# Top-32 attention and a leaky-ReLU MLP on one core: the order of the queries, the engines of the masks and the pairing of heads are changed

## The chip, the core and the metric

The kernel runs on one core of a Trainium2 chip, in one launch. The metric is the device time of an execution in microseconds (us); smaller is better. Three executions of the kernel before took 2387.86, 2389.12 and 2391.31 us, so the median is 2389.12 us. The engines are named as in the profile: PE (TensorE matmul) and PEld (its weight loads), DVE (VectorE), ACT (ScalarE), POOL (GpSimd), SP (SyncE, which issues the DMAs here).

## What is computed

All data are float32, except that the two MLP weights arrive as float64 and are rounded to float32 on the chip.

```python
# q, k, v: (8 batches, 8 heads, 576 rows, 64)
scores = (1 / sqrt(64)) * q @ k.T                   # 576 x 576 for each head
kth    = the 32nd largest of each row
scores = where(scores >= kth, scores, -1e9)
attn   = exp(scores - max);  attn = attn / (sum(attn) + 1e-9)
x      = (attn @ v), heads side by side             # 4608 tokens x 512
h      = x @ w_in                                   # 512 x 2048
out    = max(0.01 * h, h) @ w_out                   # 2048 x 512
```

## The kernel before

A pair is two neighbouring heads of a batch; there are 32 pairs, four to a batch, and a pair fills 128 rows of x. The queries of a pair (2 x 576 rows) are cut into nine tiles of 128 rows, 288 tiles in all; the middle tile (t == 4) holds 64 rows of either head. For each tile `softmax_tile` makes the scores on PE (L140: the contraction is 64 long, in two halves of 288 keys), copies them out on ACT (L147, tile s_sb), and finds the 32 largest of each row on DVE: four times MAX8 (L155) and between them three times MATCH_REPLACE8 (L160), which overwrites the eight just found. Each step needs the one before. ACT takes the exponents (L158); DVE masks and sums them in one instruction (L166) and makes the reciprocal (L171, L173); ACT scales the row (L174).

`transpose_tile` turns a tile over on PE, four blocks of 128 keys (L181) and one of 64 (L183), and ACT copies them to wT (L185, L186). When a head is complete, `weigh_values` multiplies it with v, in two halves of 288 queries and five chunks of keys (L196), and ACT copies the result into x (L203).

The tiles of two batches make a group (72 tiles, 1152 tokens). `mlp` works on a complete group in chunks of 384 tokens: for each of 16 blocks of d_ff, four matmuls (L212), a copy by ACT (L217), and the leaky ReLU by DVE (L218); then for each 128 tokens 16 matmuls (L225), a copy (L232) and a store. It is a generator, and the main loop takes its steps in even parts between the tiles of the next group, so the MLP runs a whole group behind, and the last group's MLP has no attention beside it.

A float32 matmul is two passes on PE, so counts of matmuls in the profile are twice those of the code (transposes are one pass).

The weights are loaded in 32 chunks of 128 x 512 during the first group, one to every two tiles, and rounded by `convert_weights`, ten DVE instructions to a chunk (L97 to L108). The loads of q, k and v of the next pair (six DMAs) and the stores are issued by SP. The order of each engine's instructions is chosen by the framework's scheduler from the program's dependencies and priorities; the code fixes none.

Of the kernel before, what the change touches and what calls it, by code (L numbers as in the profile page):

```python
# [8 lines left out]
F32 = mybir.dt.float32  # L9
# [3 lines left out]


@with_exitstack
def kernel(
# [4 lines left out]
    v: bass.AP,  # L21
# [7 lines left out]
    NPAIR, D, _, S = qT.shape  # L29
    B, H = v.shape[0], v.shape[1]  # L30
    DFF, DMODEL = moe_w_out.shape[0], moe_w_in.shape[0]
    P = 128
# [4 lines left out]
    assert D == 64 and S == 576 and H % 2 == 0 and DMODEL == H * D  # L37

    HS = S // 2  # a row of scores is two halves, one PSUM bank each
    NKC = 5  # chunks of keys: four of 128 and one of 64  # L40
    KLEN = [P, P, P, P, S - 4 * P]
    TPP = 2 * S // P  # 128-row query tiles of a pair; the middle one holds rows of both heads
    HP = H // 2  # pairs of a batch = 128-row chunks of d_model
    NFC = DFF // P
    GB = 2  # batches of a token group
    GTOK = GB * S
    CHT = 384  # tokens of an MLP chunk
    NGRP = B // GB
    TILES_PER_GROUP = GB * HP * TPP
    WCH = 512  # columns of a chunk of weights  # L50
    LAG = 2  # tiles by which the transposes run behind the scores
# [3 lines left out]
    loads = ctx.enter_context(tc.tile_pool(name="loads", bufs=2))  # L55
    work = ctx.enter_context(tc.tile_pool(name="work", bufs=2))
    small = ctx.enter_context(tc.tile_pool(name="small", bufs=4))
    ps_sc = ctx.enter_context(tc.tile_pool(name="ps_sc", bufs=2, space=bass.MemoryType.PSUM))
# [8 lines left out]
    gT = [const.tile([P, CHT], F32, name=f"gT{f}") for f in range(NFC)]  # L67

    def weight_chunks():
        """(destination, source) of 128 rows and 512 columns each"""  # L70
        words = moe_w_in.shape[1] // DFF
        for c in range(HP):
            for j in range(DFF // WCH):
                yield (w_in[c][:, j * WCH:(j + 1) * WCH],
                       moe_w_in[c * P:(c + 1) * P, j * WCH * words:(j + 1) * WCH * words])
        for f in range(NFC):
            for j in range(DMODEL // WCH):
                yield (w_out[f // 4][:, f % 4, j * WCH:(j + 1) * WCH],
                       moe_w_out[f * P:(f + 1) * P, j * WCH * words:(j + 1) * WCH * words])

    def load_weights(dst, src):
        """Starts a chunk's load; what convert_weights takes, if it has yet to be rounded."""
# [3 lines left out]
        raw = loads.tile([P, WCH, 2], U32, name="raw")  # L86
# [3 lines left out]
    def convert_weights(dst, raw):  # L90
        """float64 words to the nearest float32: the sign, the exponent and the leading 23 bits
        of the mantissa by bits, then the other 29 bits added as a float. Past float32's range
        it gives no finite number, and below its least normal one something below that."""
        lo, hi, bits = raw[:, :, 0], raw[:, :, 1], dst.bitcast(U32)
        ex = work.tile([P, WCH], U32, name="ex", tag="tmp")
        rem = work.tile([P, WCH], U32, name="rem", tag="tmp")
        nc.vector.tensor_scalar(ex, hi, 20, 0x7FF, ALU.logical_shift_right, ALU.bitwise_and)  # L97
        nc.vector.tensor_scalar(ex, ex, 896.0, 1151.0, ALU.max, ALU.min)
        nc.vector.tensor_scalar(ex, ex, -896.0, 8388608.0, ALU.add, ALU.mult)
        nc.vector.tensor_scalar(bits, hi, 3, 0x7FFFF8, ALU.logical_shift_left, ALU.bitwise_and)  # L100
        nc.vector.scalar_tensor_tensor(out=bits, in0=lo, scalar=29, in1=bits,
                                       op0=ALU.logical_shift_right, op1=ALU.bitwise_or)
        nc.vector.tensor_tensor(bits, bits, ex, ALU.bitwise_or)
        nc.vector.tensor_scalar(rem, lo, 0x1FFFFFFF, None, ALU.bitwise_and)
        nc.vector.scalar_tensor_tensor(out=ex.bitcast(F32), in0=rem, scalar=2.0 ** -52,  # L105
                                       in1=ex.bitcast(F32), op0=ALU.mult, op1=ALU.mult)
        nc.vector.tensor_tensor(dst, dst, ex.bitcast(F32), ALU.add)
        nc.vector.scalar_tensor_tensor(out=bits, in0=hi, scalar=0x80000000, in1=bits,  # L108
                                       op0=ALU.bitwise_and, op1=ALU.bitwise_or)

    def load_pair(pi):
        b, h0 = divmod(2 * pi, H)
        qt = loads.tile([D, 2, S], F32, name="qt")
        kt = loads.tile([D, 2, S], F32, name="kt")
        vt = loads.tile([P, 2, NKC, D], F32, name="vt")
        nc.sync.dma_start(qt, qT[pi])
        nc.sync.dma_start(kt, kT[pi])
        for side in range(2):
            nc.sync.dma_start(
                vt[:, side, 0:4, :],  # L120
                v[b, h0 + side, 0:4 * P, :].rearrange("(c p) d -> p c d", p=P),
            )
            nc.sync.dma_start(vt[0:KLEN[4], side, 4, :], v[b, h0 + side, 4 * P:S, :])
        return qt, kt, vt

    def tile_parts(t):
        """(head of the pair, first query, first row of the tile, rows)"""
        if t < 4:
            return [(0, P * t, 0, P)]
        if t == 4:  # L130
            return [(0, 4 * P, 0, 64), (1, 0, 64, 64)]
        return [(1, 64 + P * (t - 5), 0, P)]

    def softmax_tile(pair, t):
        """Normalized top-k weights of one tile of queries, [query, key]."""
        qt, kt, _ = pair
        psc = ps_sc.tile([P, 2, 512], F32, name="psc")
        for side, q0, r0, rows in tile_parts(t):
            for half in range(2):
                nc.tensor.matmul(  # L140
                    psc[r0:r0 + rows, half, 0:HS],
                    qt[:, side, q0:q0 + rows],
                    kt[:, side, half * HS:(half + 1) * HS],
                    start=True, stop=True,
                )
        s_sb = work.tile([P, S], F32, name="s_sb")
        nc.scalar.copy(s_sb.rearrange("p (h n) -> p h n", h=2), psc[:, :, 0:HS])  # L147

        tops = small.tile([P, TOPK // 8, 8], F32, name="tops")
        rest = work.tile([P, S], F32, name="rest", bufs=1)  # L150
        nbias = small.tile([P, 1], F32, name="nbias")
        e_sb = work.tile([P, S], F32, name="e_sb")
        src = s_sb
        for r in range(TOPK // 8):
            nc.vector.max(out=tops[:, r, :], in_=src)  # L155
            if r == 0:
                nc.vector.tensor_scalar(nbias, tops[:, 0, 0:1], -SCALE, None, ALU.mult)  # L157
                nc.scalar.activation(e_sb, s_sb, AF.Exp, bias=nbias, scale=SCALE)  # L158
            if r + 1 < TOPK // 8:
# [169 lines left out]
```

## Time and profile before

| | |
|---|---|
| executions | 2387.86, 2389.12, 2391.31 us (median 2389.12) |
| profiled execution, first to last instruction | 2387.1 us |
| PE busy | 2090.5 us (88%) |
| DVE busy | 1996.9 us (84%) |
| ACT busy | 984.9 us (41%) |
| POOL busy | 0.7 us |
| mean granted PE clock | 0.890 of full speed |

The profile gives the profiled execution's span and no separate time for it; the three timed executions are 0.8 to 4.2 us longer than that span. Busy time is the union of an engine's instructions; an instruction's mean duration is longer than the distance to the next one's start, since neighbours overlap at their ends. [...]

### The profile page before, as it was taken

The numbers are of one execution on the slowest core, as the hardware profiler recorded it, in microseconds if no ns is written. First come the engines' busy times: TensorE is split into PE (matmuls) and PEld (weight loads), VectorE is DVE, ScalarE is ACT, GpSimd is POOL, SyncE is SP. The second block draws the span as 40 slices with busy tenths as digits, with TensorE's granted clock in tenths as the row PEclk, the third lists the DMA queues.
The fourth block names the chain that finished last, engine by engine and source line by source line (L and its number), as shares of the span: only waits on it lengthen the run. The fifth ranks groups of instructions, "written<-read, shape, count | busy, mean of one in ns | idle before, by whom it ended". The sixth has DMA issues, their size and how long they took to land.

```text
span 2387.1 us, 21604 instructions
## 1 busy us (share of the span) xinstructions
PE 2090.5 (88%) x6688; PEld 1051.6 (44%) x6688; DVE 1996.9 (84%) x4832; ACT 984.9 (41%) x1861; POOL 0.7 (0%) x6
## 2 busy tenths in 40 slices
PE   5665666568999999999999999996899999986999
PEld 2232332234445454454454545543444545543554
DVE  8999998998889898888898898998898888998200
ACT  3333333334444454444444444444444444443110
POOL 0000000000000000000000000000000000000000
PEclk9665665557999999999999999996899999996999
DMA  3111111110000000000001000010000000000000
GB/s 77 38 42 45 42 41 41 45 42 5 20 24 16 19 20 20 24 15 15 20 16 29 13 22 20 16 28 15 10 16 24 16 24 18 17 14 0 0 14 13
DMA packets 53939, 55.93 MB, mean 23 GB/s; under 512 B 41024, under 2 KB 41024, under 8 KB 53824
## 3 DMA queue, kind: packets, MB, share of 16 engines
q1 hardware_dynamic: 53824, 54.54, 8.4%
q8 instruction: 54, 0.88, 0.2%
q14 instruction: 61, 0.50, 0.1%
HBM read 45.09 MB, written 9.44 MB: 23 GB/s over the span
## 4 chain that ended last, share of the span: by engine, by line
PE 67%; DVE 29%; ACT 3%; issue 1%; DMA 0%; DVEq 0%; SPq 0%; ACTq 0%
PE pz L225 20%; PE ph L212 15%; PE po L196 15%; PE psc L140 11%; DVE tops L155 11%; DVE rest L160 8%; PE main L181 4%; DVE w_sb L166 4%; ACT s_sb L147 1%; PE tail L183 1%; DVE gT L218 1%; DVE ex L105 1%; ACT h_sb L217 1%; ACT e_sb L158 0%; ACT wT L185 0%
## 5 line engine op out<-in xcount | busy, mean ns | idle before, releaser
L140 PE MATMUL psc<-kt,qt 64*128 64x288 f32 (+1 forms) x1280 | 459.0, 496 | 266.7 <-ACT s_sb L147 259.3
L155 DVE MAX8 tops<-rest 128x8 f32<-128x576 f32 x864 | 650.8, 753 | 12.7
L212 PE MATMUL ph<-x,w_in 128*128 128x384 f32 x1536 | 536.8, 493 | 2.9 <-ACT x L203 1.9
L225 PE MATMUL pz<-w_out,gT 128*128 128x512 f32 x1152 | 534.7, 601 | 0.0
L140 PEld LDWEIGHTS psc<-kt,qt 64*128 64x128 f32 (+1 forms) x1280 | 220.7, 203 | 492.6 <-ACT s_sb L147 354.2
L160 DVE MATCH_REPLACE8 rest<-tops,rest 128x576 f32<-128x576 f32 x576 | 427.7, 743 | 0.0
L196 PE MATMUL po<-wT,vt 128*64 128x288 f32 (+1 forms) x1280 | 397.6, 457 | 9.8 <-ACT wT L185 9.7
L212 PEld LDWEIGHTS ph<-x,w_in 128*128 128x128 f32 x1536 | 277.2, 190 | 202.0 <-issue 40.8
L147 ACT COPY s_sb<-psc 128x576 f32<-128x576 f32 x288 | 184.1, 639 | 401.7 <-DVE w_sb L166 393.0
L155 DVE MAX8 tops<-s_sb 128x8 f32<-128x576 f32 x288 | 216.7, 752 | 105.9 <-ACT s_sb L147 105.7
L225 PEld LDWEIGHTS pz<-w_out,gT 128*128 128x128 f32 x1152 | 204.6, 190 | 224.8 <-issue 206.3
L174 ACT ACTIVATE w_sb<-w_sb,rz 128x576 f32<-128x576 f32 x288 | 223.3, 775 | 168.9 <-DVE rz L173 168.0
L196 PEld LDWEIGHTS po<-wT,vt 128*64 128x64 f32 (+1 forms) x1280 | 169.7, 149 | 245.3 <-issue 124.0
L185 ACT COPY wT<-main 128x512 f32<-128x512 f32 (+1 forms) x320 | 173.2, 541 | 226.6 <-PE main L181 226.4
L218 DVE SCALAR_TENSOR_TENSOR gT<-h_sb 128x384 f32<-128x384 f32 x192 | 106.1, 553 | 189.2 <-ACT h_sb L217 187.6
L166 DVE SCALAR_TENSOR_TENSOR w_sb<-s_sb,tops,e_sb 128x576 f32<-128x576 f32 x288 | 235.1, 816 | 21.1
L158 ACT ACTIVATE e_sb<-s_sb,nbias 128x576 f32<-128x576 f32 x288 | 223.3, 775 | 40.9 <-DVE nbias L157 40.6
L181 PE MATMUL main<-ident,w_sb 128*128 128x128 f32 x1152 | 213.0, 315 | 13.4 <-ACT w_sb L174 13.1
L181 PEld LDWEIGHTS main<-ident,w_sb 128*128 128x128 f32 x1152 | 150.5, 158 | 156.8 <-ACT w_sb L174 82.3
L160 DVE MATCH_REPLACE8 rest<-tops,s_sb 128x576 f32<-128x576 f32 x288 | 213.9, 743 | 0.0
L217 ACT COPY h_sb<-ph 128x384 f32<-128x384 f32 x192 | 91.9, 479 | 177.0 <-PE ph L212 176.3
L203 ACT COPY x<-po 64x288 f32<-64x288 f32 x128 | 50.3, 393 | 268.0 <-PE po L196 267.7
(32 smaller groups left out, 624.8 us busy)
## 6 DMA issues: line engine op xcount, KB each, us to landing
qt<-in_qT_dram SPq DMA_DIRECT2D x32, 288.0 KB, 3.7
kt<-in_kT_dram SPq DMA_DIRECT2D x32, 288.0 KB, 4.5
out_dram<-o_sb SPq DMA_DIRECT2D x36, 256.0 KB, 2.0
vt<-in_v_dram SPq DMA_DIRECT2D x64, 128.0 KB, 2.3
raw<-in_moe_w_in_dram SPq DMA_DIRECT2D x16, 512.0 KB, 3.8
raw<-in_moe_w_out_dram SPq DMA_DIRECT2D x16, 512.0 KB, 3.6
vt<-in_v_dram SPq DMA_DIRECT2D x64, 16.0 KB, 2.1
```

The costliest lines, as they stand in the source:

```text
L140: nc.tensor.matmul(psc[r0:r0 + rows, half, 0:HS], qt[:, side, q0:q0 + rows], kt[:, side, half * HS:(half + 1) * HS], start=True, stop=True,)
L147: nc.scalar.copy(s_sb.rearrange("p (h n) -> p h n", h=2), psc[:, :, 0:HS])
L155: nc.vector.max(out=tops[:, r, :], in_=src)
L158: nc.scalar.activation(e_sb, s_sb, AF.Exp, bias=nbias, scale=SCALE)
L160: nc.vector.match_replace(out=rest, in_to_replace=tops[:, r, :], in_values=src, imm_value=LOWEST)
L166: nc.vector.scalar_tensor_tensor(out=w_sb, in0=s_sb, scalar=tops[:, TOPK // 8 - 1, 7:8], in1=e_sb, op0=ALU.is_ge, op1=ALU.mult, accum_out=z,)
L174: nc.scalar.activation(w_sb, w_sb, AF.Copy, bias=0.0, scale=rz)
L181: nc.tensor.transpose(main[:, c, :], w_sb[:, c * P:(c + 1) * P], ident)
L185: nc.scalar.copy(wT[side][:, 0:4, q0:q0 + rows], main[:, :, r0:r0 + rows])
L196: nc.tensor.matmul(po[rows, :], vt[0:KLEN[c], side, c, :], wT[side][0:KLEN[c], c, half * HS:(half + 1) * HS], start=(c == 0), stop=(c == N ...
L212: nc.tensor.matmul(ph[:, 0:CHT], w_in[c][:, f * P:(f + 1) * P], x[c][:, t0:t0 + CHT], start=(c == 0), stop=(c == HP - 1),)
L225: nc.tensor.matmul(pz[:, 0:DMODEL], gT[f][:, i * P:(i + 1) * P], w_out[f // 4][:, f % 4, :], start=(f == 0), stop=(f == NFC - 1),)
```

## The change

The work is now in 144 units of two tiles, one for each head of a pair, with the same 128 queries; the last 64 queries of a batch (the first, in every second batch) make units of two pairs with 64 rows each. The units go by blocks of queries, with the four pairs of a batch inside, so that 128 tokens of x are complete after every four units. The MLP works on chunks of 256, ten times 384, 256, 128 and 128 tokens, each as soon as its tokens are complete.

Unit s passes through four steps of the loop: scores in step s-1, top-k in step s, mask, exponents and normalization in step s+1, transposes, values and x in step s+2. Everything stands in `tc.manual_schedule()`: each engine works in the order of the code. Five calls of `mlp_steps` in every step put MLP work between; each adds 1720 columns to a budget and takes MLP matmuls until it is used up or no chunk is ready.

Scores of the two heads use the upper and the lower 64 rows of the PE array, and go to two PSUM tiles; values of the two heads use its two column halves. Keys are cut into chunks of 115, 115, 115, 115 and 116. The scores are masked by two POOL instructions to a tile (compare and multiply, then add), ACT takes the exponents with their sum and normalizes in place, the leaky ReLU is one ACT instruction (Prelu) out of PSUM. The rounding of weights is spread over DVE, POOL and ACT, four chunks to a step. q and k of a pair lie on 128 partitions, v is laid out by key on the host; each is one DMA, and six pairs are held at once.

```diff
+    CHUNKS = [256] + [384] * 10 + [256, 128, 128]
+    LOADED = 6
...
     def convert_weights(dst, raw):
...
         nc.vector.tensor_scalar(ex, hi, 20, 0x7FF, ALU.logical_shift_right, ALU.bitwise_and)
+        nc.vector.tensor_scalar(man, hi, 0xFFFFF, None, ALU.bitwise_and)
+        nc.gpsimd.tensor_scalar(ex, ex, 1151.0, 896.0, ALU.min, ALU.max)
+        nc.scalar.activation(frac, lo, AF.Copy, bias=1.0, scale=2.0 ** -52)
+        nc.scalar.activation(ex, ex, AF.Copy, bias=-896.0 * 2.0 ** 23, scale=2.0 ** 23)
+        nc.vector.scalar_tensor_tensor(out=frac, in0=man, scalar=2.0 ** -20, in1=frac,
+                                       op0=ALU.mult, op1=ALU.add)
+        nc.vector.scalar_tensor_tensor(out=ex, in0=hi, scalar=0x80000000, in1=ex,
                                        op0=ALU.bitwise_and, op1=ALU.bitwise_or)
+        nc.gpsimd.tensor_tensor(dst, frac, ex.bitcast(F32), ALU.mult)
...
+    def scores(u):
+        ps = [ps_sc.tile([P, 2, 512], F32, name=f"psc{i}") for i in range(2)]
+        for n in range(0, len(u.parts), 2):
+            for half in range(2):
+                for i, pi, side, r0 in u.parts[n:n + 2]:
+                    qt, kt = qk_of[pi]
+                    d = slice(side * D, (side + 1) * D)
+                    nc.tensor.matmul(
+                        ps[i][r0:r0 + u.rows, half, 0:HS],
+                        qt[d, u.q0:u.q0 + u.rows],
+                        kt[d, half * HS:(half + 1) * HS],
+                        start=True, stop=True,
+                    )
...
+            s_sb = work.tile([P, S], F32, name=f"s_sb{i}", bufs=4)
+            nc.scalar.copy(s_sb.rearrange("p (h n) -> p h n", h=2), ps[i][:, :, 0:HS])
...
+    def top_k(u):
...
+        for r in range(ROUNDS):
+            for i in range(2):
+                nc.vector.max(out=u.tops[:, i, r, :], in_=src[i])
+            if r + 1 < ROUNDS:
+                for i in range(2):
+                    nc.vector.match_replace(out=rest[i], in_to_replace=u.tops[:, i, r, :],
+                                            in_values=src[i], imm_value=LOWEST)
+                src = rest
+            yield
+
+    def mask(u):
...
+            nc.gpsimd.tensor_scalar(pen, u.s[i], u.tops[:, i, ROUNDS - 1, 7:8], MASKED,
+                                    ALU.is_lt, ALU.mult)
+            nc.gpsimd.tensor_tensor(u.s[i], u.s[i], pen, ALU.add)
+
+    def exponents(u, i):
+        nc.scalar.activation(u.s[i], u.s[i], AF.Exp, bias=u.nbias[:, i:i + 1], scale=SCALE,
+                             accum_out=u.z[:, i:i + 1])
+
+    def reciprocals(u):
...
+        nc.gpsimd.tensor_scalar(ze, u.z, 1e-9, None, ALU.add)
+        nc.vector.reciprocal(u.rz, ze)
...
+    def weigh_values(u):
...
+            for c in range(NKC):
+                for side, i in ((0, i0), (1, i1)):
+                    r0 = LEFT * side if n < P else 0
+                    nc.tensor.matmul(
+                        po[side * D:(side + 1) * D, o, :],
+                        vt[0:KLEN[c], c, side, :],
+                        u.wT[0:KLEN[c], i, c, r0:r0 + n],
+                        start=(c == 0), stop=(c == NKC - 1),
+                    )
...
+    def mlp(ch):
...
+            nc.scalar.activation(gT[f][:, 0:n], ph[:, 0:n], AF.Prelu, alpha=SLOPE)
+            yield 4 * max(n, 225)
...
+                if f % 4 == 3 and f + 1 < NFC:
+                    yield 4 * DMODEL
...
+    BUDGET = 1720
+
+    def mlp_steps(budget=BUDGET):
+        owed[0] += budget
+        while owed[0] > 0:
+            if running[0] is None:
+                if not ready:
+                    owed[0] = 0.0
+                    return
+                running[0] = mlp(ready.pop(0))
+            cost = next(running[0], None)
+            if cost is None:
+                running[0] = None
+            else:
+                owed[0] -= cost
...
+        for s in range(len(units) + 3):
+            cur, new, old, older = unit(s), unit(s + 1), unit(s - 1), unit(s - 2)
+            picks = top_k(cur) if cur else iter(())
...
+            if old:
+                mask(old)
+            next(picks, None)
+            if new:
+                scores(new)
+            convert()
+            mlp_steps()
+            next(picks, None)
+            if older:
+                transpose_main(older, 0)
+            mlp_steps()
+            if older:
+                transpose_main(older, 1)
+            convert()
+            mlp_steps()
+            next(picks, None)
+            if older:
+                transpose_tail(older)
+            if old:
+                exponents(old, 0)
+            mlp_steps()
+            if old:
+                exponents(old, 1)
+                reciprocals(old)
+            if older:
+                weigh_values(older)
+                attended(older)
+            mlp_steps()
+            next(picks, None)
+            if old:
+                normalize(old, 0)
+                normalize(old, 1)
+            load_more(s)
+        mlp_steps(1e9)
```

`convert()` rounds two chunks and fetches the next two while any are left; `attended` puts a chunk on the list `ready` when its last unit is through.

## Rows read from the trace of the kernel before

**Rows 1.** The page: span, busy time of the engines, granted clock in 40 slices.

```profile
span 2387.1 us, 21604 instructions
PE 2090.5 (88%) x6688; PEld 1051.6 (44%) x6688; DVE 1996.9 (84%) x4832; ACT 984.9 (41%) x1861; POOL 0.7 (0%) x6
...
PEclk9665665557999999999999999996899999996999
```

**Rows 2.** Windows by stage: us, busy of PE, PEld, DVE, ACT, POOL, PEclk, DMA share, GB/s.

```profile
0.00:562.00 562.00, 341.32 (x912) 167.14 (x913) 521.13 (x1284) 191.63 (x362) 0.70 (x6) 0.65 0.16 44
562.00:1156.00 594.00, 587.34 (x1984) 295.56 (x1984) 521.82 (x1259) 280.05 (x528) 0.00 (x0) 1.00 0.07 19
...
2218.00:2387.00 169.00, 165.34 (x450) 84.06 (x448) 17.87 (x32) 19.63 (x40) 0.00 (x0) 1.00 0.03 10
```

**Rows 3.** Waits, 100 to 560 us: us in total, times, longest.

```profile
PEld psc L140 <- ACT s_sb L147: 197.5, 44, 5.9
```

**Rows 4.** Timeline of PE, last group's MLP: start, length, passes.

```profile
2328.75 13.39 PE L212 MATMUL ph<-x,w_in 128*128 128x384 f32 x41
...
2341.98 41.36 PE L225 MATMUL pz<-w_out,gT 128*128 128x512 f32 x96
```

**Rows 5.** Timeline of PE, scores of two middle tiles (t == 4).

```profile
906.34 1.19 PE L140 MATMUL psc<-kt,qt 64*64 64x288 f32 x8
...
971.13 1.18 PE L140 MATMUL psc<-kt,qt 64*64 64x288 f32 x4
```

**Rows 6.** Timeline of PE around 1200 us: transposes, values.

```profile
1202.26 0.60 PE L181 MATMUL main<-ident,w_sb 128*128 128x128 f32 x4
...
1204.19 5.49 PE L196 MATMUL po<-wT,vt 128*64 128x288 f32 x20
```

**Rows 7.** Timeline of DVE around 1208 us: starts of neighbours.

```profile
1207.74 0.76 DVE L155 MAX8 tops<-rest 128x8 f32<-128x576 f32 x1
1208.42 0.14 DVE L173 RECIPROCAL rz<-ze 128x1 f32<-128x1 f32 x1
...
1209.14 0.07 DVE L160 MATCH_VALUE_LOAD rest<-tops,rest 128x8 f32 x1
1209.20 0.74 DVE L160 MATCH_REPLACE8 rest<-tops,rest 128x576 f32<-128x576 f32 x1
1209.86 0.14 DVE L157 TENSOR_SCALAR nbias<-tops 128x1 f32<-128x1 f32 x1
```

**Rows 8.** Groups by line and shape: busy us, mean ns | idle before.

```profile
L166 DVE SCALAR_TENSOR_TENSOR w_sb<-s_sb,tops,e_sb 128x576 f32<-128x576 f32 x288 | 235.1, 816 | 21.1
...
L158 ACT ACTIVATE e_sb<-s_sb,nbias 128x576 f32<-128x576 f32 x288 | 223.3, 775 | 40.9 <-DVE nbias L157 40.6 <-ACT w_sb L174 0.3
...
L218 DVE SCALAR_TENSOR_TENSOR gT<-h_sb 128x384 f32<-128x384 f32 x192 | 106.1, 553 | 189.2 <-ACT h_sb L217 187.6
...
L105 DVE SCALAR_TENSOR_TENSOR ex<-rem,ex 128x512 f32<-128x512 uint32 x32 | 21.8, 681 | 0.0
L97 DVE TENSOR_SCALAR ex<-raw 128x512 uint32<-128x512 uint32 x32 | 13.4, 417 | 9.6 <-DMA raw<-in_moe_w_in_dram 9.6
```

**Rows 9.** Groups by line and shape, POOL.

```profile
masks.py:199 POOL TENSOR_SCALAR_AFFINE_SELECT ident<-ident 128x128 f32<-128x128 f32 x1 | 0.3, 294 | 0.1
masks.py:197 POOL MEMSET ident<- 128x128 f32 x1 | 0.2, 205 | 0.3 <-POOLq L316 0.3
...
L316 POOL MEMSET const-float32-0.0<- 128x1 f32 x1 | 0.1, 99 | 0.2 <-issue 0.2
```

**Rows 10.** The page, DMA issues: KB each, median us to landing.

```profile
raw<-in_moe_w_in_dram SPq DMA_DIRECT2D x16, 512.0 KB, 3.8
```

**Rows 11.** Timeline of PE, the first matmuls.

```profile
6.60 8.02 PE L140 MATMUL psc<-kt,qt 64*128 64x288 f32 x16 [6.60 <-DMA kt<-in_kT_dram]
```

**Rows 12.** Windows around the start of the second group (columns as in rows 2).

```profile
556.00:563.00 7.00, 6.31 (x16) 2.80 (x17) 6.16 (x15) 1.44 (x4) 0.00 (x0) 0.53 0.00 0
563.00:570.00 7.00, 6.01 (x21) 2.88 (x21) 3.40 (x9) 3.26 (x7) 0.00 (x0) 1.00 0.20 45
```

More of the change, by code (lines that the diff above doesn't have):

```diff
@@ L85, in load_weights @@
             return None
[L86 removed]
+        raw = raws.tile([P, WCH, 2], U32, name="raw")
         nc.sync.dma_start(raw.rearrange("p n w -> p (n w)"), src)
@@ L124, in load_pair, with load_v @@
[L124 to L138, printed above, removed]
-            for half in range(2):
+        qk_of[pi] = qt, kt
+    def load_v(pi):
+        v_of[pi] = loads.tile([KMAX, NKC, 2, D], F32, name="vt")
+        nc.sync.dma_start(v_of[pi], vk[pi])
@@ new lines, with x_at @@
+    x_of = {}
+    def x_at(token):
+        c = 0
+        while token >= CHUNKS[c]:
+            token -= CHUNKS[c]
+            c += 1
+        return c, token
+    def weigh_values(u):
+        n = u.rows
+        po = ps_tr.tile([P, len(u.outs), n], F32, name="po", tag="tr")
+        for o, (pi, i0, i1) in enumerate(u.outs):
+            vt = v_of[pi]
+            for c in range(NKC):
[7 more added lines that the diff above has]
+                    )
+        ch, col = x_at(u.b * S + u.q0)
+        if ch not in x_of:
+            x_of[ch] = [xpool.tile([P, CHMAX], F32, name=f"x{c}") for c in range(HP)]
+        for o, (pi, _, _) in enumerate(u.outs):
+            nc.scalar.copy(x_of[ch][pi % HP][:, col:col + n], po[:, o, :])
@@ L140, in softmax_tile @@
+    def mlp(ch):
+        n = CHUNKS[ch]
+        t0 = sum(CHUNKS[:ch])
+        x = x_of[ch]
+        for f in range(NFC):
+            ph = ps_ml.tile([P, 512], F32, name="ph", tag="ml")
+            for c in range(HP):
                 nc.tensor.matmul(
[L141 to L144, printed above, removed]
-                )
-        s_sb = work.tile([P, S], F32, name="s_sb")
@@ L147, in softmax_tile @@
[L147 to L159, printed above, removed]
-                nc.vector.match_replace(out=rest, in_to_replace=tops[:, r, :],
-                                        in_values=src, imm_value=LOWEST)
-                src = rest
@@ L188, in weigh_values @@
[L188 to L195 removed]
+                    ph[:, 0:n], w_in[c][:, f * P:(f + 1) * P], x[c][:, 0:n],
+                    start=(c == 0), stop=(c == HP - 1),
+                )
+            nc.scalar.activation(gT[f][:, 0:n], ph[:, 0:n], AF.Prelu, alpha=SLOPE)
@@ new lines, in unit, with attended, fetch_weights @@
+    def unit(n):
+        return units[n] if 0 <= n < len(units) else None
+    done_tokens = [0] * len(CHUNKS)
+    def attended(u):
+        ch, _ = x_at(u.b * S + u.q0)
+        done_tokens[ch] += u.rows * len(u.pairs)
+        if done_tokens[ch] == CHUNKS[ch] * HP:
+            ready.append(ch)
+    chunks, raw_chunks = weight_chunks(), []
+    def fetch_weights():
+        chunk = next(chunks, None)
+        got = load_weights(*chunk) if chunk else None
+        if got:
+            raw_chunks.append(got)
@@ new lines, with load_more, convert @@
+    with tc.manual_schedule():
+        last = {p: n for n, u in enumerate(units) for p in u.pairs}
+        load_qk(0)
+        scores(units[0])
+        for _ in range(2):
+            fetch_weights()
+        def load_more(s):
+            for of, load, lag in ((qk_of, load_qk, -1), (v_of, load_v, 2)):
+                while len(of) < NPAIR and (len(of) < LOADED or last[len(of) - LOADED] + lag <= s):
+                    load(len(of))
+        load_more(-1)
+        for s in range(len(units) + 3):
+            cur, new, old, older = unit(s), unit(s + 1), unit(s - 1), unit(s - 2)
+            picks = top_k(cur) if cur else iter(())
+            def convert():
+                for _ in range(2):
+                    if raw_chunks:
+                        convert_weights(*raw_chunks.pop(0))
+                    fetch_weights()
+            if old:
[32 more added lines that the diff above has]
+        mlp_steps(1e9)
```

255 lines of the change are left out of this document (94 added, 161 removed).

## The prediction, made before any run of the change

> **What bounds the kernel now.** I first read the page [rows 1]: PE is busy 88% of the span and DVE 84%, so neither can be the limit everywhere, and the clock line shows half speed in most of the first quarter. The windows by stage [rows 2] separate the cases. In the first group, 562 us without MLP, DVE is busy 521 us and PE 341 us at a mean clock of 0.65: DVE is the limit there, and PE waits for it (its weight loads lost 197.5 us of 460 to score copies held up behind DVE [rows 3]). From 562 to 1156 us PE is busy 587 of 594 us at full clock: with the MLP beside the attention, PE is the limit. The last 169 us are MLP alone. So the question for the change is what PE and DVE need per unit, and whether both are kept busy at the same time. All sums below are made against the span of 2387.1 us; the median of the executions, 2389.12, is 2.0 us more.
>
> **What a unit costs after the change.** DVE: a top-k instruction that need not wait for its neighbour starts 0.66 to 0.68 us after it, and the value load takes 0.06 us [rows 7]. The change puts the other head's instruction between each two that depend on each other, so I use these distances: 8 MAX8 x 0.67 + 6 x (0.06 + 0.66) + a reciprocal of 0.07 = 9.75 us for two tiles. Gone from DVE are the masking instruction, 816 ns a tile, and the leaky ReLU, 106 us in all [rows 8].
>
> PE, at full clock: eight passes of scores in the two column halves of the array took 1.19 us in one place, and four passes in a single half 1.18 us in another [rows 5]. So passes on different parts of the array do run together. The trace shows this for column halves only; the change pairs row halves for scores and column halves for values. I take both as pairing fully. Scores: 1.15 us. Transposes: four took 0.60 us with the last one's tail, so ten at 0.11 are 1.1 us [rows 6]. [...] Sum 3.65 us. If neither pair ran together, scores would cost 1 us more and values 1.2 us more.
>
> MLP, unchanged in work: 41 passes of 384 columns in 13.39 us, 96 of 512 in 41.36 us [rows 4], so a chunk of 384 tokens (128 and 96 passes) costs 41.8 + 41.4 = 83.2 us, or 1.69 us per 1000 columns of the budget (a chunk counts 49,152).
>
> ACT (41% busy now) gains 64 short instructions for the weights and loses small copies; Prelu takes the copy's place. Nothing in the sum goes by it. Its cover is the time DVE and PE need anyway, 9.75 us against some 6 to 8 us of ACT per step.
>
> **POOL.** The trace has no such operation on it. One-input instructions over 128 columns took 205 and 294 ns, over one column 99 [rows 9]: 0.83 to 1.53 ns a column, hence 0.58 to 0.98 us for 576. For the two-input add I take at least 0.98 and at most twice that slope, 1.86. Values taken: 0.8 and 1.4, in the middle, for neither end is nearer. A unit's masks: 4.6 us, bounds 3.3 to 5.9. [...] Masks are covered if POOL's 4.6 us, an exponent (0.78 [rows 8]) and the small steps to the reciprocal (0.5) end before DVE's third round, 8.3 us after the step began: 5.9 us, so yes, and at the upper bound (7.2) still.
>
> **The order decides the sum.** DVE has one reciprocal in each step, behind the third round, and it needs the exponents, which on ACT stand behind the Prelu of the fourth `mlp_steps`. PE's transposes of the next step need the normalized row. So DVE, ACT and PE go through the steps together, and cannot lead by more than part of one. Each step takes the longer of DVE's 9.75 us and PE's 3.65 us plus its MLP. Five calls of 1720 are 8600 columns, 14.5 us: while MLP is ready, a step takes PE 18 us and DVE idles; a chunk of 49,152 is then used up in 5.7 steps, though its successor is ready only after 12. So PE idles in the others. Counting `mlp_steps` through the code for one chunk: 3072 columns, five steps with 41,984 together, 4096, then five with none.
>
> Cycle of 12 steps: five full ones 71.1 + 5 x 3.65 = 89.3; the part steps 9.75 and 6.9 + 3.65 = 10.6; five empty ones 48.8; and the clock. In the empty steps PE has little to do, as in the first group, where the clock was mostly half; at the start of the second group PE was busy 6.31 of 7 us at 0.53 before it had 1.00 [rows 12]. I count 4 us lost at each start of MLP (bounds 0 and 7). Cycle: 162.5 us.
>
> **Head.** Scores start at 6.6 us [rows 11]: 7. Steps 0 to 7 round four weight chunks each. DVE's share per chunk is two short (417 ns) and two long (681 ns) instructions [rows 8], but the second long one waits for a chain: long (0.68), POOL's product of the chunk before (1.25), POOL's clamp (0.7), an ACT scaling (0.6), gaps 0.15 = 3.4 us a chunk, during which DVE's queue, with the next top-k round, stands still. (With POOL's bounds 2.8 to 4.2.) A step: 9.75 + 13.6 = 23.4; eight: 187. SP's queue is passed by all loads, but a fetch of 512 KB lands 3.8 us after issue [rows 10] and has some 6 us until its turn; nothing. The six loads of a pair become three, for pairs needed many units later; nothing.
>
> **Sum.** Head 7 + 187; steps 8 and 9 empty 19.5; chunk 0 (256 tokens, 55.5 us) in four steps, with attention and clock 71; seven empty steps 68; nine full cycles 1462; the tenth chunk 114 and one empty step 9.75; steps 137 to the end: chunks of 256, 128 and 128, 111 us, with the last attention 30, clock 4, last copy and store 3. Together 2086. In the stage where PE was the limit it still idled 1.1% [rows 2]; that adds 20. With 2 us outside the span I forecast **2108 us**, 12% less than before. Its own bounds: 2040 with a fast POOL and no loss of clock; 2290 with both pairings failing in the some 75 steps that PE limits.
>
> **Rivals.**
> A: *DVE leads enough that bursts cost nothing.* Then PE works on without a break after the head: 194 + 20 + 989 of MLP + 137 x 3.65 = 1703, with 1% and the drain about 1740. For it speaks that DVE needs only 138 x 9.75 = 1346 us there; against it, the reciprocal in the middle of each step. Halfway cases end near 1900. Chance 0.12.
> B: *The heads don't share the array* as scores use row halves, which no row shows: some 75 steps x 2.2 us = 165 more, 2270. Chance 0.08.
> C, slower: *POOL's instructions hold up DVE's top-k.* In every step that DVE limits (53 empty, 26 part), its 9.75 us grow by POOL's 4.6: + 363, 2470 us. It decides from 3.6 us a step on ((2389 - 2108) / 79). In the trace POOL is idle beside DVE throughout, so no row excludes it. [...] Chance 0.06.
> D: *POOL is far slower than its rows say.* From 5.2 us a tile (upper bound 2.84) the masks delay the reciprocal enough to lose all the gain; 2400 and more. Chance 0.04. A milder form, 3.6 to 5, gives 2150 to 2380: 0.05.
>
> **How the numbers follow.** Forecast 0.65, A 0.12, B 0.08, C 0.06, D 0.09 in its two forms. The range, 1920 to 2300, takes in the forecast with its bounds, B, the milder end of A and of D; A's rest, C and D's rest, some 0.18, are out. A measurement tells 0.2%, 5 us, from no change. Faster: all but C, D's slow form and a sliver near 2389: 0.88; same 0.02; slower 0.10.
>
> **What would show it.** Right: in 40 slices, DVE's digits near 9 and PE's near 5 to 7 in some, and PE 9 with DVE near 5 in others, about a dozen times in turn, the clock falling with PE's; steps of 9.8 and 18 us; POOL busy about 700 us; scores with 8 passes in 1.2 us; DVE waiting for the exponents' sums where MLP runs. Wrong: PE or DVE at 9 throughout (A), MAX8 starting over 0.8 us apart while POOL works (C), DVE's reciprocal waiting for POOL in steps without MLP (D), score passes 0.24 us apart (B), or rounding steps far from 23 us.

## The result, and the profile after

The changed kernel takes 2142.76 us (median of four executions, 2140.65 to 2146.47), beside 2388.76 for the kernel before on the same chip: a ratio of 0.8969, 95% interval 0.8956 to 0.8981. The forecast was 2108, 35 us too low, inside its range. The profiled execution spans 2138.9 us.

The page of the changed kernel, with the lines that answer to [rows 1]:

```profile
span 2138.9 us, 25069 instructions
PE 1743.4 (82%) x8864; PEld 1065.6 (50%) x8864; DVE 1496.2 (70%) x3152; ACT 975.9 (46%) x2069; POOL 1174.4 (55%) x934
...
PE   1122796897897898898898898798798799699898
...
DVE  4788859758857857857857856956955955955760
```

PE fell from 2090.5 to 1743.4 us and DVE from 1996.9 to 1496.2, but neither is busy everywhere: from the fifth slice on PE's digits swing between 6 and 9, and DVE's between 5 and 9, one high where the other is low. The windows of one chunk show it, against [rows 2] (us, busy of PE, PEld, DVE, ACT, POOL, PEclk, which is the granted clock as a share of full speed, DMA share, GB/s):

```profile
60.00:235.00 175.00, 51.16 (x266) 34.90 (x266) 146.37 (x259) 69.52 (x137) 108.52 (x95) 1.00 0.23 75
...
525.00:557.00 32.00, 22.34 (x127) 16.33 (x124) 32.00 (x72) 17.36 (x38) 25.77 (x20) 0.67 0.18 56
557.00:672.00 115.00, 110.38 (x495) 61.26 (x493) 68.63 (x148) 48.96 (x104) 53.84 (x42) 1.00 0.07 23
```

First the rounding of weights, in which DVE is the busiest engine (84%); then stretches without MLP, in which DVE is busy for all of 32 us and the granted clock is 0.67 on the mean; then bursts of MLP, in which PE is busy 96% and DVE 60%. The one reciprocal of each step is a clock for reading this. Timeline of DVE, reciprocals alone (start, length; in brackets the idle time before it and what ended that):

```profile
519.49 0.15 DVE L208 RECIPROCAL rz<-ze 128x2 f32<-128x2 f32 x1
529.19 0.15 DVE L208 RECIPROCAL rz<-ze 128x2 f32<-128x2 f32 x1
...
558.30 0.14 DVE L208 RECIPROCAL rz<-ze 128x2 f32<-128x2 f32 x1
575.92 0.17 DVE L208 RECIPROCAL rz<-ze 128x2 f32<-128x2 f32 x1 [7.85 <-POOL ze L207]
```

A step without MLP takes 9.70 us and DVE waits for nothing; steps with MLP take 14.5 to 20.8 us and DVE waits in each. Over twelve steps, six of either kind, that is 163.8 us on the mean. Timeline of PE, values and scores inside a burst, the answer to [rows 5, 6]:

```profile
611.27 1.31 PE L248 MATMUL po<-wT,vt 115*64 115x128 f32 x20
...
616.15 1.24 PE L163 MATMUL psc<-kt,qt 64*128 64x288 f32 x8
```

Both pairs share the array: 20 passes of 128 columns in 1.31 us, 8 of 288 in 1.24. The waits of the whole execution (us in total, times, longest) and POOL's groups:

```profile
POOL ze L207 <- ACT s_sb L201: 687.6, 133, 12.2
DVE rz L208 <- POOL ze L207: 548.3, 71, 11.9
...
PE main L218 <- ACT s_sb L211: 213.5, 70, 27.2
```
```profile
L196 POOL TENSOR_SCALAR pen<-s_sb,tops 128x576 f32<-128x576 f32 x288 | 641.3, 2227 | 109.3 <-DVE tops L182 108.7 <-PE ph L268 0.6
L198 POOL TENSOR_TENSOR s_sb<-s_sb,pen 128x576 f32<-128x576 f32 x288 | 405.8, 1409 | 24.0
...
L106 POOL TENSOR_SCALAR ex<-ex 128x512 uint32<-128x512 uint32 x32 | 21.4, 670 | 40.6 <-DVE ex L104 38.6
```

DVE's wait at the reciprocal, 71 times, is the lockstep of the prediction: it makes up 548 of the 643 us in which DVE is not busy. PE has the other side of it, 213.5 us of waiting for rows that ACT has still to normalize (L211). The compare-and-multiply takes 2227 ns, far outside its bounds.

### The profile page after: what moved, and what is told of

Same layout as the page of the kernel before. It is cut to its first block, busy times and chain, and to the rows that moved or that the text cites. A ratio compares the mean times of both kernels' runs of the same rounds, so it can differ in the third digit from the quotient of the medians.

```text
span 2138.9 us, 25069 instructions
## 1 busy us (share of the span) xinstructions
PE 1743.4 (82%) x8864; PEld 1065.6 (50%) x8864; DVE 1496.2 (70%) x3152; ACT 975.9 (46%) x2069; POOL 1174.4 (55%) x934
## 4 chain that ended last, share of the span: by engine, by line
PE 59%; DVE 27%; POOL 7%; ACT 4%; issue 1%; DMA 1%; SPq 0%; POOLq 0%; ACTq 0%; DVEq 0%
PE ph L268 23%; PE pz L277 23%; DVE tops L182 14%; DVE rest L185 12%; PE psc L163 4%; PE main L218 4%; PE po L248 4%; POOL pen L196 3%; POOL s_sb L198 2%; ACT s_sb L201 1%; DVE ex L111 1%; POOL ex L106 1%; ACT ex L108 1%; DMA raw<-in_moe_w_in_dram 1%; PE tail L225 1%
## 5 line engine op out<-in xcount | busy, mean ns | idle before, releaser
L196 POOL TENSOR_SCALAR pen<-s_sb,tops 128x576 f32<-128x576 f32 x288 | 641.3, 2227 | 109.3 <-DVE tops L182 108.7
L268 PE MATMUL ph<-x,w_in 128*128 128x384 f32 (+2 forms) x1792 | 543.7, 451 | 7.5 <-ACT x L258 7.5
L198 POOL TENSOR_TENSOR s_sb<-s_sb,pen 128x576 f32<-128x576 f32 x288 | 405.8, 1409 | 24.0
L218 PE MATMUL main<-ident,s_sb 128*115 128x128 f32 x1152 | 218.6, 334 | 213.5 <-ACT s_sb L211 213.5
L218 PEld LDWEIGHTS main<-ident,s_sb 128*115 128x115 f32 x1152 | 190.8, 224 | 304.4 <-ACT s_sb L211 226.3
L201 ACT ACTIVATE s_sb<-s_sb,nbias 128x576 f32<-128x576 f32 x288 | 222.8, 777 | 207.8 <-POOL s_sb L198 207.8
L248 PE MATMUL po<-wT,vt 115*64 115x128 f32 (+3 forms) x3200 | 250.1, 320 | 43.9 <-ACT wT L226 36.7
L248 PEld LDWEIGHTS po<-wT,vt 115*64 115x64 f32 (+1 forms) x3200 | 208.0, 173 | 104.9 <-ACT wT L226 39.1
L163 PE MATMUL psc<-kt,qt 64*128 64x288 f32 (+1 forms) x1280 | 222.7, 474 | 34.4 <-ACT s_sb L172 27.0
L211 ACT ACTIVATE s_sb<-s_sb,rz 128x576 f32<-128x576 f32 x288 | 207.2, 768 | 53.6 <-DVE rz L208 53.6
```

The source lines that it names most:

```text
L163: nc.tensor.matmul(ps[i][r0:r0 + u.rows, half, 0:HS], qt[d, u.q0:u.q0 + u.rows], kt[d, half * HS:(half + 1) * HS], start=True, stop=True,)
L196: nc.gpsimd.tensor_scalar(pen, u.s[i], u.tops[:, i, ROUNDS - 1, 7:8], MASKED, ALU.is_lt, ALU.mult)
L198: nc.gpsimd.tensor_tensor(u.s[i], u.s[i], pen, ALU.add)
L201: nc.scalar.activation(u.s[i], u.s[i], AF.Exp, bias=u.nbias[:, i:i + 1], scale=SCALE, accum_out=u.z[:, i:i + 1])
L211: nc.scalar.activation(u.s[i], u.s[i], AF.Copy, bias=0.0, scale=u.rz[:, i:i + 1])
L218: nc.tensor.transpose(main[0:KLEN[c], c, :], u.s[i][:, c * KSTEP:c * KSTEP + KLEN[c]], ident)
```

## Where the head's time went

By its own terms the forecast put the first reciprocal, which stands in step 1 behind three rounds and four weight chunks, at 7 + 23.4 + 8.3 + 13.6 = 52.3 us and the seventh, in the last step of rounding, at 52.3 + 6 x 23.4 = 192.7; they came at 70.7 and 226.7. Behind that the forecast had 2106 - 193 = 1913 us left and the trace 2138.9 - 226.7 = 1912. So the miss lies in the head (behind it two errors offset each other, as the last part tells), and two stretches explain it. DVE and SP in step 0:

```profile
35.77 0.43 DVE L104 TENSOR_SCALAR ex<-raw 128x512 uint32<-128x512 uint32 x1 [14.27 <-DMA raw<-in_moe_w_in_dram]
```
```profile
10.40 9.91 SPq L128 DMA_DIRECT2D vt<-in_vk_dram  x6
20.43 18.32 SPq L93 DMA_DIRECT2D raw<-in_moe_w_in_dram  x3
```

Six loads of v, needed two steps later, stand in SP's queue ahead of the next weight fetches, and DVE waits 14.3 us. The place in the queue is the smaller part of this: the first of these fetches was issued at 20.43 us, and DVE had its data at 35.77, 15.3 us after the issue, where [rows 10] had 3.8. Windows with q, k and the first weights under way, then with v alone (columns as above):

```profile
6.00:12.00 6.00, 3.07 (x12) 1.28 (x9) 3.54 (x8) 1.18 (x2) 0.72 (x1) 1.00 1.02 393
16.00:24.00 8.00, 0.00 (x0) 0.00 (x0) 5.24 (x9) 0.63 (x1) 2.52 (x3) 1.00 0.26 103
```

The loads of v keep the DMA engines busy for 0.26 of the time and move 103 GB/s, about a quarter of the 393 before, so they are still under way when the fetch is issued. v lies on 116 partitions, q, k and the weights on 128; whether that is why v is slow no run here tells.

And a rounding step takes 26.0 us, where the forecast had 23.4. DVE, then POOL, at the first two weight chunks of one such step:

```profile
153.54 0.41 DVE L105 TENSOR_SCALAR man<-raw 128x512 uint32<-128x512 uint32 x1
154.05 0.96 DVE L109 SCALAR_TENSOR_TENSOR frac<-man,frac 128x512 f32<-128x512 uint32 x1
158.82 0.69 DVE L111 SCALAR_TENSOR_TENSOR ex<-raw,ex 128x512 uint32<-128x512 uint32 x1 [3.80 <-ACT ex L108]
...
159.77 1.49 DVE L105 TENSOR_SCALAR man<-raw 128x512 uint32<-128x512 uint32 x1
```
```profile
153.31 2.63 POOL L196 TENSOR_SCALAR pen<-s_sb,tops 128x576 f32<-128x576 f32 x1
156.03 1.40 POOL L198 TENSOR_TENSOR s_sb<-s_sb,pen 128x576 f32<-128x576 f32 x1
157.51 0.61 POOL L106 TENSOR_SCALAR ex<-ex 128x512 uint32<-128x512 uint32 x1
159.60 1.38 POOL L113 TENSOR_TENSOR w_out<-frac,ex 128x512 f32<-128x512 f32 x1 [1.47 <-DVE ex L111]
```

The clamp of the first chunk stands in POOL's queue behind four mask instructions; ACT's scaling waits for the clamp and DVE for that, 3.80 us. The four chunks take 6.6, 3.6, 2.5 and 3.6 us, and 16.3 + 9.7 = 26.0.

## The experiments

The theory is the prediction's: a step takes the longer of DVE's 9.7 us and PE's attention plus its MLP, so a burst wastes DVE and an empty step PE. Its chief rival is A, that DVE leads enough for the order not to matter. Times without an interval are of one execution.

**The size of the burst.** With the even run's edit below, a step takes 4100 columns of MLP. The control has the new CHUNKS and xpool lines but BUDGET 1720; the third run has BUDGET 3440 alone.

```diff
-    CHUNKS = [256] + [384] * 10 + [256, 128, 128]
+    CHUNKS = [256] * 17 + [128, 128]
...
-    xpool = ctx.enter_context(tc.tile_pool(name="xpool", bufs=2))
+    xpool = ctx.enter_context(tc.tile_pool(name="xpool", bufs=3))
...
-    BUDGET = 1720
+    BUDGET = 820
```

Even, 820:

> Edit: BUDGET 820 instead of 1720 (five calls put 4100 columns of MLP, 6.9 us, into each step), with MLP chunks of 256 tokens and a third x buffer, which so slow an MLP needs; the work is the same. Theory (lockstep: each step takes the longer of DVE's 9.75 us and PE's attention plus its MLP, so bursts waste DVE and empty steps waste PE): steps of 10.6 us by the sum, 10 to 12 with waits, nearly all alike; head 250 us, 137 steps x 11 = 1507, drain 20, together about 1780 (1700 to 1860), PE at full clock after the head. Rival (DVE leads enough that bursts already cost nothing; the rest is POOL or waits that every step has): no change, 2140 within 30. Rival (an evenly but not fully loaded PE is granted the half clock): steps of 14 us and more, 2150 to 2400.

Control, 1720 with chunks of 256:

> Edit: chunks of 256 tokens and the third x buffer alone, BUDGET stays 1720. It is the control for the even budget. Theory (lockstep): a chunk's columns and its steps shrink alike, about four full steps and four empty ones to a chunk of eight, so 2140 within 50. Rival (chunk size or the buffer is what helps): the time goes down as far as in the run with 820.

Larger bursts, 3440:

> Edit: BUDGET 3440 instead of 1720, chunks as in the change. Theory (lockstep): a full step takes PE 3.65 + 29 = 33 us, a chunk is used up in three steps, nine are empty: cycle 83 + 3 x 3.65 + 9 x 9.7 = 181 instead of 163, over 10 cycles + 180 us, 2320 (2280 to 2370). Rival (DVE leads far enough): no change, 2140 within 20.

Measured: 1775.91 us with 820 (ratio to the kernel before 0.7423, interval 0.7402 to 0.7444), 2155.8 for the control, 2348.1 with 3440. The theory had 1780, 2140 and 2320. Same work, some 570 us apart, by its distribution (the control's other two lines are worth 13): rival A is wrong, and neither the chunk size nor the third buffer is what helps. Reciprocals with 3440, then with 820:

```profile
439.73 0.17 DVE L208 RECIPROCAL rz<-ze 128x2 f32<-128x2 f32 x1 [23.90 <-POOL ze L207]
...
499.98 0.17 DVE L208 RECIPROCAL rz<-ze 128x2 f32<-128x2 f32 x1 [21.58 <-POOL ze L207]
509.69 0.15 DVE L208 RECIPROCAL rz<-ze 128x2 f32<-128x2 f32 x1
```
```profile
1002.29 0.17 DVE L208 RECIPROCAL rz<-ze 128x2 f32<-128x2 f32 x1 [0.82 <-POOL ze L207]
1012.81 0.17 DVE L208 RECIPROCAL rz<-ze 128x2 f32<-128x2 f32 x1 [0.72 <-POOL ze L207]
```

With 3440, steps of 29 to 34 us and nine of 9.7, 181 us a cycle as forecast; the rest of the miss is in the shorter chunks at the ends. With 820 a step is 10.8 us on the mean and DVE waits under 1 us in most. A window of the even run from 400 to 1600 us:

```profile
400.00:1600.00 1200.00, 1192.89 (x7247) 818.99 (x7246) 1087.93 (x2334) 722.98 (x1595) 853.64 (x668) 1.00 0.07 23
```

PE is busy 99% at full clock, so the rival of a half clock is wrong too, and in this stretch PE is now the limit.

**The cover of the masks.**

```diff
             nc.gpsimd.tensor_tensor(u.s[i], u.s[i], pen, ALU.add)
+            nc.gpsimd.tensor_tensor(u.s[i], u.s[i], pen, ALU.add)
```

> Edit: POOL's add of the mask is issued twice for each tile, the second with the same operands, so masked scores get the penalty twice, which leaves their exponents at zero. It adds 2 x 1.41 = 2.8 us of POOL to a step. Theory (the masks are just covered in steps without MLP: the sum reaches POOL about when DVE's third round ends): those steps grow from 9.7 to 12.4 us, about 60 of them, + 160; rounding steps + 20; full steps nothing; 2300 in all (2260 to 2360). Rival (the masks have several us of cover left): under + 40.

Measured: 2374.3 us, 232 more. A reciprocal in a step without MLP, one of many alike (the step before it ended 12.53 us sooner):

```profile
565.56 0.17 DVE L209 RECIPROCAL rz<-ze 128x2 f32<-128x2 f32 x1 [2.73 <-POOL ze L208]
```

Of 2.82 us added DVE waits 2.7, so the change's masks have about 0.1 us of cover left. The direction was right, the time 14 us above the range and 74 above the 2300 expected: 66 steps, not 60, and the first step of most bursts grew too (to 19 to 21 us, from 17.6 to 18.3).

**The pairing of values.** One column half for both heads, and for that two copies into x instead of one.

```diff
-        po = ps_tr.tile([P, len(u.outs), n], F32, name="po", tag="tr")
+        po = ps_tr.tile([D, len(u.outs), 2, n], F32, name="po", tag="tr")
...
-            for c in range(NKC):
-                for side, i in ((0, i0), (1, i1)):
+            for side, i in ((0, i0), (1, i1)):
+                for c in range(NKC):
...
-                        po[side * D:(side + 1) * D, o, :],
+                        po[:, o, side, :],
...
```

> Edit: the values of the two heads use one column half of the PE array, one head after the other (and two copies into x instead of one); the rest is the change. Theory (column halves run together): 20 passes of 128 columns take 2.4 us instead of the 1.31 seen, + 1.1 us in the some 70 steps that PE limits, nothing in the steps of 9.7 us: + 75, 2215 (2190 to 2240). Rival (the passes wait for wT or po whichever half they use): no change, within 10.

Measured: 2213.4 us, 71 more. The timeline of PE in a burst has

```profile
623.54 2.40 PE L248 MATMUL po<-wT,vt 115*64 115x128 f32 x20
```

and each step of a burst after its first grew by 1.1 us, those without MLP by nothing. So column halves run together, and the limits lie in the steps where the theory has them.

**Masks back on DVE.**

```diff
-            nc.gpsimd.tensor_scalar(pen, u.s[i], u.tops[:, i, ROUNDS - 1, 7:8], MASKED,
-                                    ALU.is_lt, ALU.mult)
-            nc.gpsimd.tensor_tensor(u.s[i], u.s[i], pen, ALU.add)
...
+        nc.scalar.activation(u.e[i], u.s[i], AF.Exp, bias=u.nbias[:, i:i + 1], scale=SCALE)
+        nc.vector.scalar_tensor_tensor(
+            out=u.s[i], in0=u.s[i], scalar=u.tops[:, i, ROUNDS - 1, 7:8], in1=u.e[i],
+            op0=ALU.is_ge, op1=ALU.mult, accum_out=u.z[:, i:i + 1])
```

> Edit: masks and sums back on DVE, one two-input instruction a tile behind ACT's exponent (compare, multiply, sum), none on POOL; the rest is the change. Theory (steps without MLP are DVE's, full steps PE's, and the rounding's first clamp waits behind POOL's masks): steps of 9.7 us become 9.7 + 2 x 0.82 + 0.6 for the wait at the reciprocal = 11.9, 64 x 2.2 = + 140; a rounding step + 2.2 - 4, 7 x -1.8 = -13; full steps the same; 2270 in all (2220 to 2310). Rival (POOL's 7.5 us of masks already limit those steps): they stay at 9.7 or shrink, and the time does not rise.

Measured: 2229.1 us, 86 more, so the move to POOL pays, slow as POOL is. Steps without MLP take 11.68 us, with 0.41 of waiting:

```profile
525.81 0.17 DVE L206 RECIPROCAL rz<-ze 128x2 f32<-128x2 f32 x1 [0.41 <-POOL ze L205]
537.49 0.17 DVE L206 RECIPROCAL rz<-ze 128x2 f32<-128x2 f32 x1 [0.41 <-POOL ze L205]
```

They gave 66 x 2.0 = + 130. The expectation missed that the first step of a burst would shrink, by some 2.5 us each; rounding steps fell to 23.9.

**The two causes in the head.** First the loads of v:

```diff
-                while len(of) < NPAIR and (len(of) < LOADED or last[len(of) - LOADED] + lag <= s):
+                while len(of) < NPAIR and (s >= 0 if of is v_of and len(of) < LOADED else
+                                           len(of) < LOADED or last[len(of) - LOADED] + lag <= s):
```

> Edit: the loads of v of the first six pairs are issued at the end of step 0, behind the weight fetches, instead of ahead of them. Theory (the second pair of weight fetches stands behind six loads of v in SP's queue, DVE waits 14.3 us for it in step 0): that wait goes to under 6 us, the first reciprocal comes 9 to 14 us sooner (at 57 to 62 us, not 70.7), everything behind it is the same; 2131 (2127 to 2136). Rival (the fetches land late because the transfers themselves share the DMA engines): the first reciprocal moves by less than 3 us.

Measured: 2133.8 us, the first reciprocal at 61.0. The 14.3 us are gone from step 0; 4.1 come back in step 1. SP, then DVE:

```profile
28.43 6.23 SPq L128 DMA_DIRECT2D vt<-in_vk_dram  x6
41.55 17.07 SPq L93 DMA_DIRECT2D raw<-in_moe_w_in_dram  x4
```
```profile
40.84 0.69 DVE L111 SCALAR_TENSOR_TENSOR ex<-raw,ex 128x512 uint32<-128x512 uint32 x1 [3.80 <-ACT ex L108]
...
52.05 0.43 DVE L104 TENSOR_SCALAR ex<-raw 128x512 uint32<-128x512 uint32 x1 [4.14 <-DMA raw<-in_moe_w_in_dram]
```

Here nothing stood ahead of the fetch in SP's queue: the last load of v was issued by 34.7 us, and the fetch at 41.55, as soon as DVE had let go of its buffer (40.84 + 0.69). DVE still had its data only 10.5 us later, beside v's transfers. In step 0, with v out of the way, a fetch issued at 15.55 us was there when DVE asked for it at 21.82. So moving the loads helps, but the run cleared the queue and the DMA engines of them at once. By these times the rival's cause, the shared DMA engines, is the larger part, though its forecast for this run was wrong; no run parts the two. Then the clamp:

```diff
-        nc.gpsimd.tensor_scalar(ex, ex, 1151.0, 896.0, ALU.min, ALU.max)
+        nc.vector.tensor_scalar(ex, ex, 1151.0, 896.0, ALU.min, ALU.max)
```

> Edit: in the rounding of weights the clamp is on DVE instead of POOL; the product stays on POOL. Theory (in each rounding step the first clamp stands behind four mask instructions in POOL's queue, so DVE's first chunk takes 6.6 us where the next three take 3.6, 2.5 and 3.6): the first chunk falls to 3 to 4 us, the other three stay within 0.4, the step falls from 26.0 to 23 (22 to 24), over some seven steps and the last chunks -22, 2121 (2112 to 2130). Rival (POOL's masks hold up DVE's two-input instructions directly, wherever the clamp is): the first chunk stays over 5.5 us and the time within 8 of 2143.

Measured: 2125.3 us, steps of 23.46. The four chunks take 3.2, 4.7, 2.4 and 3.5 us: the first fell as expected, the second grew by 1.1, a miss, for DVE now reaches it while POOL still adds masks. DVE, then POOL, there:

```profile
144.98 1.65 DVE L104 TENSOR_SCALAR ex<-raw 128x512 uint32<-128x512 uint32 x1
```
```profile
144.95 1.40 POOL L198 TENSOR_TENSOR s_sb<-s_sb,pen 128x576 f32<-128x576 f32 x1
```

**What is slow about POOL's compare.** Two runs replace it, with another form for each head.

The first run's two forms stand where the change has its one:

```diff
+            if i == 0:
+                nc.gpsimd.tensor_scalar(pen, u.s[i], u.tops[:, i, ROUNDS - 1, 7:8], 0.0,
+                                        ALU.subtract, ALU.mult)
+            else:
+                nc.gpsimd.tensor_scalar(pen, u.s[i], 0.0, MASKED, ALU.is_lt, ALU.mult)
```

> Edit: POOL's first mask instruction in two forms that split the present one (compare with a per-row scalar, then multiply by a constant, 2.23 us). Head 0: subtract the per-row scalar, multiply by 0 (no compare; masks nothing). Head 1: compare with the constant 0, multiply (no per-row scalar; masks the negative scores instead of all but 32). Theory (the compare is what is slow on POOL, as the clamp, also two operations but with constants and without a compare, takes 0.67 us for 512 columns): head 0 about 0.75 us, head 1 about 2.2. Rival (the per-row scalar is slow): head 0 2.2, head 1 0.75. Rival (neither: float32 at 576 columns in this form costs 2.2): both 2.2. In all three, steps without MLP stay at 9.7 us, since the masks are covered there; where one form is fast, 1.5 us come off each rounding step's first clamp: 2133 (2126 to 2143).

The second run's:

```diff
+            if i == 0:
+                nc.gpsimd.tensor_scalar(pen, u.s[i], 1151.0, -1151.0, ALU.min, ALU.max)
+            else:
+                nc.gpsimd.tensor_scalar(pen, u.s[i], u.tops[:, i, ROUNDS - 1, 7:8], None, ALU.is_lt)
```

> Edit: POOL's first mask instruction in two other forms, 2.23 us in the change. Head 0: the clamp's two operations (minimum, then maximum, with constants) on float32 (masks nothing, the scores are doubled). Head 1: one operation only, the compare with the per-row scalar (adds 1 to the scores below the 32nd largest, which masks nothing). Theory A (multiplying and comparing are what is slow, minimum and maximum are not): head 0 about 0.75 us, head 1 about 2.2 or somewhat less. Theory B (two operations on float32 cost twice one; the clamp of the weights is fast for its integer operands): head 0 about 2.2, head 1 about 1.2. Theory C (any such float32 instruction costs this): both 2.2. Steps without MLP stay at 9.7 us in all; the rounding step falls by what the two instructions save, so at most some 2.5 us for each of seven: 2143 under C, 2125 to 2138 under A and B.

POOL's groups of the first run (subtract with a per-row scalar, then compare with a constant), and of the second (compare alone, then minimum and maximum):

```profile
L197 POOL TENSOR_SCALAR pen<-s_sb,tops 128x576 f32<-128x576 f32 x144 | 319.8, 2221 | 109.0 <-DVE tops L182 107.6 <-PE ph L271 1.4
L200 POOL TENSOR_SCALAR pen<-s_sb 128x576 f32<-128x576 f32 x144 | 308.5, 2143 | 12.0
```
```profile
L199 POOL TENSOR_SCALAR pen<-s_sb,tops 128x576 f32<-128x576 f32 x144 | 249.0, 1729 | 162.3 <-DVE tops L182 159.2 <-PE ph L271 2.5
L197 POOL TENSOR_SCALAR pen<-s_sb 128x576 f32<-128x576 f32 x144 | 96.1, 667 | 9.0
```

Neither the compare nor the per-row scalar is the cause by itself: without the compare the instruction still takes 2221 ns, without the per-row scalar 2143. Minimum and maximum with constants take 667 ns, where compare and multiply with constants, on the same float32 tile, take 2143, and the compare alone takes 1729. So the price hangs on the operations, not on the type or on their number (theory A of the second run). Whether a multiplication alone is slow was not tried. Times: 2141.3 and 2110.0 us; the second is 33 less than the change, more than expected. Rounding steps fell from 26.0 to 22.5 us, for head 0's instruction no longer waits for the 32nd largest either, and the head ended 24 us sooner; the rest came off the first steps of bursts. Steps without MLP stayed at 9.7 in both.

**Together.** The even budget, v later and the clamp on DVE, by the edits above; in one of the two runs the product is on DVE as well.

> Edit: the even budget (820, chunks of 256, third x buffer) with the loads of v later and the rounding's clamp and product both on DVE. Theory: the parts add up: 1776 - 9 (v later) - 7 x 2.7 (rounding steps of 23.3 us, since the product adds 4 x 0.6 to DVE, and the 1.07 us that an instruction beside POOL's product lost is saved twice) = 1748 (1738 to 1758); steps after the head as before, 10.75 on the mean. Rival (with an even budget PE is the limit and a shorter head only moves a wait): within 5 of 1776.

> Edit: as the run with clamp and product on DVE, but the product stays on POOL. Theory: 1776 - 9 - 7 x 2.5 = 1749 (1740 to 1758), rounding steps of 23.5 us as with the clamp alone; the two runs differ by less than 8 us. Rival as there.

Measured: 1755.62 with the product on DVE (steps of 24.1, not 23.3: one of its four products took 1.79 us beside POOL's masks), 1750.62 with the product on POOL, ratio 0.7325 to the kernel before (0.7313 to 0.7336), 18% below the change. In the latter the parts add up (1749 expected); the former came out 8 above its 1748, by those steps. Windows of the latter:

```profile
0.00:230.00 230.00, 76.40 (x379) 52.75 (x380) 208.94 (x383) 93.70 (x181) 122.28 (x97) 0.99 0.30 97
230.00:1690.00 1460.00, 1448.69 (x8814) 990.68 (x8813) 1304.84 (x2802) 877.29 (x1935) 1030.53 (x806) 1.00 0.07 23
```

What is left is a head in which DVE is busy 91% and 1460 us that PE fills (99%).

## Why the prediction was right, and where it was off

- **DVE, 9.75 us a unit**: 9.70. The distance between the starts of independent instructions [rows 7], not their lengths, was the right price.
- **PE, 3.65 us a unit**: in the even run 10.8 us less 6.9 for 4100 columns leave 3.9. Row halves pair as column halves do (8 passes in 1.24 us, where [rows 5] had 4 passes in a single half in 1.18), so rival B is wrong. The sum of 3.65 has 1.4 us in it for the values, which no run shows; the trace has 1.31 us for their 20 passes.
- **Lockstep through the reciprocal**: that the engines go through the steps together is shown by the size of the burst. That the reciprocal is what ties them is read from the waits; no run takes it away, so what would hold DVE next stays open. The cycle of 162.5 us with 1.1% on top is 164.3; the trace has 163.8. Inside it the clock was mis-sized. PE's first MLP passes of a chunk, and eight at full clock in the same burst:

```profile
554.82 2.98 PE L268 MATMUL ph<-x,w_in 128*128 128x384 f32 x6
...
571.54 2.75 PE L268 MATMUL ph<-x,w_in 128*128 128x384 f32 x8
```

  Six passes took 0.9 us more than six of the later ones (2.1), so the start, at a granted clock of 0.50 until 556 us, costs about 1 us where the forecast had 4. The six steps with MLP took 105.6 us, where it had 99.9 and those 4. So PE's own part was nearly 5 us too low and the clock 3 too high; with the 1.1% they offset each other, and that the stretch behind the head came out within 1 us is in part luck.
- **POOL, 0.8 us for the compare, bounds 0.58 to 0.98**: 2.23. The rows taken for it [rows 9] were other operations, and the runs show 0.67 to 2.2 us for the same tile by operation alone. With the add (1.41, forecast 1.4) a tile costs 3.64 us, where the prediction's rival D began to cost time at 3.6. So D's premise came true: POOL was busy 1174 us where the sign for being right was about 700. Yet the masks kept 0.1 us of cover, instead of the 2.4 that 8.3 less 5.9 would leave, and the steps without MLP stayed at 9.7 us. That the sum held here was luck.
- **Head, 23.4 us a step**: 26.0. The chain of 3.4 us a chunk was about right for the second and the fourth (3.6) and too long for the third (2.5); for the first it left out that POOL's clamp is queued behind the masks, whose 7.3 us of POOL the change had just moved there. Seven steps by 2.6 are 18 us of the head's 34.
- **Loads, nothing**: 14.3 us. The prediction gave a fetch 3.8 us from issue to landing and some 6 until its turn; at the start six loads of v are ahead of it, first in SP's queue and then in the DMA engines, and it took 15.3 us from its issue alone. With the 18 us this leaves 2 of the 34 unnamed.
- **Rival C** (its chance of 0.06 was the author's estimate): the top-k is not held up. MAX8's groups, in the change and in the kernel before, where POOL is idle:

```profile
L182 DVE MAX8 tops<-rest 128x8 f32<-128x576 f32 x864 | 607.9, 745 | 0.0
```
```profile
L155 DVE MAX8 tops<-rest 128x8 f32<-128x576 f32 x864 | 650.8, 753 | 12.7
```

  DVE's rounding is held up: L105 takes 0.42 us by itself and 1.49 beside POOL's product. Not all of it is: the two-input L109 ran from 154.05 to 155.01 us inside POOL's compare (153.31 to 155.94), 0.96 us where its mean is 0.91. Which instructions of the two engines hold each other up, and by what, no run here shows.
- **Slips in the sums**: a unit's masks, 4.6 us, are 0.2 more than 2 x (0.8 + 1.4); chunk 0's 71 us leave under 1 us for the clock, not 4; rival A's 989 us of MLP would be 998 by the price of 83.2 us for 384 tokens. None of them moves the forecast by more than 3 us.

## What to carry to other kernels

Where a fixed order ties engines to one step, the time is the sum over steps of the slowest engine in each, and totals by engine say little: the same work took 2348, 2143 or 1776 us by how its MLP was spread. So size the background work to use up a step's slack, no more. When work is moved to an idle engine, read what already waits in that engine's queue for something short, and measure the operation itself there rather than a neighbour of it.

## What the runs showed of the hardware

- On POOL a tile of 128 x 576 float32 took 667 ns for minimum and maximum, 1729 for a compare, 2143 to 2227 for a compare or a subtraction with a multiplication, and 1409 for adding two tiles.
- DVE's one-input rounding instructions (0.41 us) took 1.49 to 1.65 us where a two-input POOL instruction had just begun. Beside POOL's compare L105 kept 0.41, and the two-input L109 took 0.96 (its mean is 0.91); the clamp, in the run that moved it to DVE, took 0.88 there and 0.41 elsewhere. The compare took 2.63 us instead of 2.22 in either run.
- While only the loads of v were under way, the DMA engines were busy 0.26 of the time and moved 103 GB/s; with q, k and weights under way they were busy throughout (a share of 1.02) and moved 393.
- Two passes of a float32 matmul on different halves of the array ran together with rows of the array split (1.24 us for 8 of 288, where four in a single half took 1.18) as with columns (1.31 us for 20 of 128, 2.40 in a single half).
